# A recorded order of an attention and MLP kernel: three loads for half of a q, and other places for loads, RELUs and copies

## The chip, the cores and the metric

The kernel runs on one core of a Trainium2 chip. The metric is the device time of one execution in microseconds (us), the median of three runs. All products are in bf16 on TensorE with sums in f32; inputs and output are f32 in the chip's main memory.

## What is computed

Two parts, one behind the other. The first is attention without a softmax, for 8 batches of 12 heads, 448 positions and 64 features. The second is an MLP with exact GELU on the 3584 rows that come out.

```python
scores = scale * np.matmul(q, k.transpose(0, 1, 3, 2))       # 448 x 448 for each head
attn = np.maximum(scores, 0.0) ** 2 / S
x = matmul(attn, v)                                          # heads side by side: 3584 x 768
h = x @ w_in                                                 # 768 -> 2048
out = (0.5 * h * (1 + erf(h / sqrt(2)))) @ w_out             # 2048 -> 768
```

## The kernel before

**Engines.** Five engines have instruction streams of their own: TensorE (PE), ScalarE (ACT), VectorE (DVE), GpSimd (POOL) and SyncE (SP). Here POOL issues all loads, with a conversion from f32 to bf16 on the way, in one queue (q0 of the profile). It rotates over eight semaphores, so that each of its DMAs waits for the landing of the eighth before it. SP issues the transposes of batches 2 and later, the stores, and a few copies (q1). Each engine takes its instructions strictly in order, and waits at an instruction whose input or buffer isn't ready.

**Attention.** A batch is cut into three groups of four heads, and a group into seven blocks of 128 keys. I write QK(b.g.i) for the scores of one block: four matmuls (L744, in `add_steps`, L727) into a PSUM buffer "w", of which there are three. A RELU empties that buffer into an SBUF tile a_sq, on ACT (L756) or on DVE (L758); a multiplication on DVE squares it in place (MUL, L765). When a group's seven blocks are squared, an AV (`add_av`, L790) multiplies them with v in 28 matmuls (L805), in seven steps, into another "w" buffer, and two copies bring it to xT on ACT or DVE. Batch 0 does all this in halves of the 448 queries, a and b, two half blocks to an instruction.

**Transposes.** TensorE needs q and k with the features on the partitions. For batches 0 and 1 it transposes them itself (`add_tk` L604, `add_tq` L631) and ACT or DVE copies them out of PSUM. For batches 2 to 7 the DMA engines do it (`add_T_dma`, L659, instructions at L667), and a second arrangement of q is made by two half-swap copies on DVE, or by two DMAs of SP ("qT<-qT").

**MLP.** F1 (`add_f1`, L846, matmuls L857) multiplies one column block m of w_in with xT, six matmuls each, and ACT's GELU empties it. F1 of batches 0 to 3 is done while the attention of later batches runs. The second MLP half goes in seven-product groups (`add_group`, L1148) with sums on DVE (L1170), differences of w_out (`add_tsums`, L1115, at L1120), products (L1191) and results passed on (L1225). F1 of the last four batches is done in blocks of the same kind (`add_blocks`, L1009).

**The order.** Nothing is scheduled when the kernel is built: the string `ORDER` (L86) holds every operation in turn, 1471 words. A word is an engine's letter (P, A, D, G for POOL, S) and the operation's number, counted as the operations are added; Z is a filling operation. `Scheduler.place` (L356) reads it word by word. The word thus sets the order on each engine and also, for RELUs and copies that may go to either, the engine. Whether a wait results, only the chip decides.

The loads of batch 0's q: group 0's first half is loaded ahead of everything by SP, those of groups 1 and 2 by one load each, and the second halves of all three groups by one load `add_q(0, 0, G, HC, NC)` (L1378; G is 3, HC to NC the second half).

The order of the loads in POOL's queue before (q, k, v with batch and group; a and b the halves of batch 0's q; "ident" a small instruction):

```
k0g1 q0g1a k0g2 q0g2a ident q0b(all groups) k1g1 v0g0 k1g0 v0g2 q1g0 q1g1 v0g1 win0 win1 k1g2 q1g2
win2 k2g0 win3 v1g0 win4 q2g0 k2g1 q2g2 q2g1 k2g2 v1g1 v1g2 q3g0 wout0 v2g0 wout1 v2g1 q3g1 k3g0 ...
```

win0 and win1 hold two column blocks of w_in each, win2 to win4 four each; wout0 is one half of w_out, wout1 and wout2 a quarter each. SP issues batch 2's transposes in the order q0 k0 q1 k1 q2 k2.

Of the kernel before, what the change touches and what calls it, by code (L numbers as in the profile page):

```python
# [14 lines left out]
NC = S // KC  # L15
HC = NC // 2
# [70 lines left out]
G0 G1 G3 G4 G1470 G7 A10 D13 A16 G121 P11 G2 P17 D12 D18 G117 P14 P42 D15 P39 G6 A43 P21 A40 P33  # L87
D22 P36 D44 P19 A37 P23 D20 G118 A34 D24 P25 G122 P54 D41 A26 G5 A55 P66 P57 Z1056 D67 A58 P63
P27 P29 A64 P69 D30 P48 D59 P31 A70 D28 D38 P78 A49 P51 D35 P133 G8 A52 D50 P45 D68 A79 P81 D53
A134 D46 P75 D47 G9 D65 A32 P131 A82 D56 P111 D132 A76 P108 D112 P129 G125 A109 D71 P102 P84 D103  # L90
G126 A85 P72 D80 P60 A73 D130 G120 A74 P93 D77 A61 P135 D104 A62 P96 D110 P105 A97 P141 D106 G147
A94 G124 D98 P165 A142 P90 P168 D107 A166 P143 D113 D86 A91 D83 P114 G119 A169 D92 P87 D115 A144
D95 A116 P171 D88 P137 A172 D89 P99 D138 A136 P159 P156 G128 D100 P145 D160 A157 D101 P162 A146
D173 P174 P186 G148 D175 P251 A187 D167 P243 A252 D170 A163 D158 P183 D188 A244 P189 P195 G150
P259 D184 A196 G154 A190 D176 P253 G151 D164 A260 G153 D161 P139 D191 P180 A140 P198 P177 D181
A199 D185 A254 P219 P216 G123 A178 P245 A220 G127 D179 S229 D182 P247 A246 A217 S228 P210 A248
P204 D218 P207 P263 A208 D205 P261 D211 A264 D197 S232 P192 A262 P213 D200 P222 A214 P255 D209
S231 A223 D193 P257 A256 D215 S235 P267 D206 A258 D194 S234 D221 P249 A268 D224 D212 P201 A250
P225 D230 G270 A202 A203 G238 P276 P279 A226 G149 D277 P265 A227 G239 A280 D233 P294 A266 P288
P291 A295 G152 P356 A289 P348 G272 G269 G271 P303 P285 A357 A292 A349 P350 A304 A286 P354 A351  # L100
D287 P312 P300 A355 P318 S399 P362 D281 D313 D296 P364 A363 D319 P370 D278 A301 A365 P358 A371
P315 P306 A359 P282 P352 D307 P360 A353 G241 P376 A361 P368 A377 A283 P366 A369 D284 D302 D236
D293 P372 A367 D290 P374 A373 P378 D390 D316 G274 P327 A379 P297 D391 A328 G273 G155 P333 P339
D314 A334 G240 P382 D298 D305 D317 A340 A375 S398 D308 A299 D320 D329 P330 P324 D417 P309 A325
P380 A383 A331 D310 D311 D392 P342 P321 P336 A381 A337 D332 D418 D341 D419 D326 S402 P384 A322
S401 D393 P387 D396 A385 S405 D394 D400 G407 G242 G237 A323 A343 G409 S386 G275 S404 P443 P446
D335 D420 G408 A444 P421 D395 D344 A447 D338 P449 D388 A450 D397 S389 A422 G412 P452 P345 D445
D346 P437 G411 P423 A453 A438 P440 A347 D424 D403 P455 S542 A441 P425 A456 D439 D442 P473 A426
P470 P461 P427 D454 A471 A474 D462 P429 D428 D457 P464 P479 P476 D430 A480 P431 D448 A465 D451
G414 G415 P433 D472 A477 D432 D562 D406 P467 P458 A468 S435 D469 P485 P491 S545 A486 D434 P509  # L110
D459 A492 S541 P513 A510 D560 A460 D478 D561 P503 S544 A514 P494 P500 D563 P519 A501 D481 D463
P515 A520 D475 A504 A495 D493 P517 D466 D543 S547 D496 D487 P488 A518 P482 A516 D502 S548 G552
P497 P511 D498 S436 G555 D499 P523 G551 A512 D489 A483 G550 A484 G416 P525 A524 D490 D546 G554
P600 G413 P609 P606 G410 D610 P521 D505 A601 A607 P603 P506 D604 A526 A522 P612 P639 D507 P531
A640 P527 G558 D613 D605 A532 D508 G557 P618 A528 P624 P615 D619 P529 S705 S704 A616 P537 S708
# [12 lines left out]
P832 D890 A878 P886 P904 D833 A887 S947 P690 D834 G848 G853 D905 P892 A691 P883 P692 A893 D884
D888 P901 A693 P898 P910 A911 P698 S950 D906 D882 D899 D885 D894 D876 P696 A699 S946 P694 D725
A697 S599 A902 D879 D912 P702 A695 P700 A703 D903 D726 P727 A701 D900 D891 P916 S949 P907 P895  # L130
D917 A908 A728 S948 P928 P913 D929 D909 P731 A914 S953 A896 D915 D918 P729 A897 S951 D930 P925
P922 S952 P919 D926 A923 D730 S579 P931 D927 D732 P934 A920 P733 A921 A932 D924 D935 P735 D734
D736 D933 P940 P937 P955 P737 A956 D936 D743 A941 P739 D738 A938 D744 S741 D942 P747 D939 D740
P958 A748 P970 S742 P943 D959 A971 S954 D746 P961 P964 A944 D1035 P749 A962 D965 A945 D966 P973
P982 D750 P967 P751 A974 A968 D745 D957 D969 D963 D972 P753 A752 P755 A983 D960 D754 D975 P994
P985 P976 A995 D986 P979 P997 D756 D984 P757 A980 A998 D854 D1037 P759 D987 A977 D758 A978 S761
P1015 D981 D855 P988 P1003 A1016 P858 D760 D856 D1027 A989 P860 A1004 A859 P991 P1018 P1012 D861
D999 D1036 A1019 P862 D990 D996 A992 P864 D1038 A1013 D993 D1017 P1021 P1000 D865 D1028 D1020
A1022 D857 A863 P1006 P1009 A1001 P866 A1002 A1007 D1030 D1127 D1005 P1039 P1056 P1041 A1057
# [1420 lines left out]
```

## Time and profile before

| | us |
|---|---|
| median of three runs (lowest, highest) | 366.22 (366.13, 366.34) |
| span of the profiled execution, first to last instruction | 365.2 |
| TensorE busy | 356.2 |
| VectorE busy | 297.5 |
| ScalarE busy | 208.2 |
| GpSimd busy | 64.2 |

The span leaves out what lies around the first and the last instruction, about 1.0 us against the median. In the views below, a line of groups gives the code line, the engine, the operation, output and input, a count, the busy time and the mean of one in ns, and then the idle time ahead of it with what ended it. A line of waits reads: who, waiting for whom, us in total, times, the longest. A line of a timeline or of the chain begins with its start and its length in us; xN is the number of instructions, and [0.23 <-DVE ...] an idle time ahead of it and what ended it. A row of windows gives, for a stretch of the span, the busy us of each engine with the number of its instructions in brackets, the granted clock, the DMA engines' share, and GB/s. A line of DMA issues ends with the median us from issue to landing.

### The profile page before, as it was taken

To read this page: it belongs to the slowest core of one execution; us is meant where nothing else is said; L and a number is where in the kernel's file an instruction comes from. 1 tells how busy PE (TensorE), PEld (TensorE's weight loads), DVE (VectorE), ACT (ScalarE), POOL (GpSimd) and SP (SyncE) were. 2 spreads that over 40 slices of the span, in tenths; PEclk is the share of its full clock that TensorE was granted. 3 is DMA by queue.
4 is the path that set the end of the run, shared out by engine and by line. 5 is a ranking of instruction groups with operands and counts; after the bars stand their busy time and mean duration, and the time that the engine had idled before them with its cause. 6 is when DMAs were issued, how large, how long until landed. Compare 5 with 4: busy or idle time off the path is not lost.

```text
span 365.2 us, 8578 instructions
## 1 busy us (share of the span) xinstructions
PE 356.2 (98%) x3598; PEld 225.4 (62%) x3598; DVE 297.5 (81%) x510; ACT 208.2 (57%) x337; POOL 64.2 (18%) x101
## 2 busy tenths in 40 slices
PE   8799999999999999999999999999999999999996
PEld 4575644455454445555445555799787689788664
DVE  3899784399999988999899999999867847665764
ACT  5998868555767686766766677437027024425310
POOL 8575224160124125014000000000000000000000
PEclk9999999999999999999999999999999999999999
DMA  9999999999999999999792301002021200140223
GB/s 168 199 200 207 198 154 138 191 203 181 186 221 198 197 172 209 219 157 154 132 168 70 95 20 43 3 2 86 3 85 46 88 0 2 45 129 2 85 70 106
DMA packets 73126, 44.12 MB, mean 121 GB/s; under 512 B 38144, under 2 KB 69760, under 8 KB 73088
## 3 DMA queue, kind: packets, MB, share of 16 engines
q0 software_dynamic: 32912, 22.47, 42.7%
q1 hardware_dynamic: 39280, 20.26, 29.0%
q10 hardware_dynamic: 896, 0.85, 0.7%
q8 instruction: 28, 0.46, 0.5%
q14 instruction: 10, 0.08, 0.1%
HBM read 45.61 MB, written 11.01 MB: 155 GB/s over the span
## 4 chain that ended last, share of the span: by engine, by line
PE 78%; DVE 10%; DMA 7%; POOL 2%; issue 2%; ACT 1%; POOLq 0%; DVEq 0%
PE pso L1191 33%; PE pb L1009 18%; PE psh L857 14%; PE ps L744 7%; PE pav L805 6%; DMA win_sb<-in_moe_w_in_dram 5%; DVE a_sq L765 4%; DMA nq<-in_q_dram 2%; DVE t_sb L1120 1%; DVE a_sq L758 1%; DVE s_sb L1170 1%; DVE qT L518 1%; POOL nk L553 1%; ACT a_sq L756 0%; POOL win_sb L481 0%
## 5 line engine op out<-in xcount | busy, mean ns | idle before, releaser
L756 ACT ACTIVATE a_sq<-ps 128x896 bf16<-128x896 f32 (+1 forms) x125 | 110.3, 927 | 33.5 <-PE ps L744 33.4
L765 DVE TENSOR_TENSOR a_sq<-a_sq 128x896 bf16<-128x896 bf16 (+1 forms) x169 | 96.9, 614 | 11.8 <-ACT a_sq L756 11.3
L857 PE MATMUL psh<-xT,win_sb 128*128 128x448 bf16 (+1 forms) x420 | 77.6, 337 | 0.9 <-DMA win_sb<-in_moe_w_in_dram 0.9
L857 PEld LDWEIGHTS <-win_sb 128*128 128x128 bf16 x420 | 38.9, 98 | 37.3 <-issue 9.4
L1046 DVE TENSOR_TENSOR part<-pb,part 128x448 f32<-128x448 f32 x80 | 47.3, 619 | 15.9 <-PE pb L1009 14.2
L1191 PEld LDWEIGHTS <-s_sb 128*128 128x128 bf16 x424 | 40.5, 98 | 26.8 <-issue 2.4
L758 DVE TENSOR_SCALAR a_sq<-ps 128x896 bf16<-128x896 f32 (+1 forms) x44 | 47.1, 1074 | 9.2 <-PE ps L744 9.1
L744 PE MATMUL ps<-qT,kT 64*64 64x448 bf16 (+1 forms) x756 | 47.7, 336 | 1.6 <-ACT qT L520 0.5
L867 ACT ACTIVATE h_sb<-psh 128x448 bf16<-128x448 f32 x64 | 35.0, 552 | 20.8 <-PE psh L857 20.4
L1191 PEld LDWEIGHTS <-h_sb 128*128 128x128 bf16 x312 | 29.4, 98 | 21.6 <-issue 4.6
L1009 PEld LDWEIGHTS <-win_sb 128*128 128x128 bf16 x384 | 36.8, 98 | 2.7 <-issue 0.4
L1191 PE MATMUL pso<-wout_sb,h_sb 128*128 128x384 bf16 x208 | 38.1, 326 | 0.0
L1191 PE MATMUL pso<-t_sb,s_sb 128*128 128x384 bf16 x208 | 38.1, 326 | 0.0
L1191 PE MATMUL pso<-wout_sb,s_sb 128*128 128x384 bf16 (+1 forms) x208 | 37.6, 324 | 0.0
L805 PE MATMUL pav<-a_sq,v_sb 64*64 64x448 bf16 (+1 forms) x756 | 36.7, 329 | 0.6 <-DVE a_sq L765 0.2
L1055 ACT ACTIVATE h_sb<-part 128x448 bf16<-128x448 f32 x48 | 25.4, 575 | 14.6 <-DVE part L1046 14.6
L1225 DVE TENSOR_TENSOR osb<-pso,p_sb 128x384 f32<-128x384 f32 x39 | 21.5, 552 | 14.7 <-PE pso L1191 11.0
L744 PEld LDWEIGHTS <-kT 64*64 64x64 bf16 x756 | 18.8, 105 | 22.3 <-issue 16.3
L805 PEld LDWEIGHTS <-v_sb 64*64 64x64 bf16 x756 | 21.4, 107 | 11.9 <-issue 2.5
L464 POOL DMA_DIRECT2D nq<-in_q_dram x24 | 17.8, 744 | 59.9 <-DMA qT<-nq 55.2
L1009 PEld LDWEIGHTS <-ws 128*128 128x128 bf16 x288 | 27.6, 98 | 1.0
L1055 ACT ACTIVATE h_sb<-pb 128x448 bf16<-128x448 f32 x16 | 8.2, 541 | 29.3 <-PE pb L1009 29.2
(62 smaller groups left out, 327.1 us busy)
## 6 DMA issues: line engine op xcount, KB each, us to landing
nk<-in_k_dram POOLq DMA_DIRECT2D x23, 224.0 KB, 8.1
nq<-in_q_dram POOLq DMA_DIRECT2D x21, 224.0 KB, 7.0
v_sb<-in_v_dram POOLq DMA_DIRECT2D x5, 672.0 KB, 11.6
out_dram<-osb SPq DMA_DIRECT2D x7, 336.0 KB, 2.9
v_sb<-in_v_dram POOLq DMA_DIRECT2D x9, 224.0 KB, 9.9
out_dram<-osb SPq DMA_DIRECT2D x7, 288.0 KB, 3.3
out_dram<-osb SPq DMA_DIRECT2D x8, 240.0 KB, 3.0
win_sb<-in_moe_w_in_dram POOLq DMA_DIRECT2D x8, 192.0 KB, 9.6
```

The costliest lines, as they stand in the source:

```text
L744: nc.tensor.matmul(ps[64 * j : 64 * j + 64, e, x * w : x * w + w], kT[r, g, i * 128 + 64 * j : i * 128 + 64 * j + 64], moving, start=True, ...
L756: A.activation(ar, ps, AF.Relu, scale=c_att)
L758: V.tensor_scalar(ar, ps, c_att, 0.0, op0=mybir.AluOpType.mult, op1=mybir.AluOpType.max,)
L765: V.tensor_mul(box["a2"][:, :, :used], ar, ar)
L805: nc.tensor.matmul(pav[0][o2 : o2 + 64, e, :w], vt[b][r, 2 * g + e, bass.ts(i, D)], box["a2"][r, y, o : o + w], start=(i == 0), stop=(i == ...
L857: nc.tensor.matmul(ph[:, x * n : x * n + n], win_sb[:, kd, bass.ts(m + x, 128)], xT[b][:, kd, c], start=(kd == 0), stop=(kd == KD - 1),)
L867: A.activation(h_ring()[:, m : m + nm, o + c.start : o + c.stop], box[0][:, :S].rearrange("p (x n) -> p x n", x=nm), AF.Gelu,)
L1009: nc.tensor.matmul(bank[name][:, y, z * HS : z * HS + HS], w[:, k, bass.ts(mm, 128)], right()[:, k], start=first and k == 0 and z == 0, st ...
L1046: V.tensor_add(get(to), ps(name), get(other))
L1055: A.activation(h_ring()[:, m : m + 2, o + half[c].start : o + half[c].stop], src().rearrange("p (x n) -> p x n", x=2), AF.Gelu,)
L1191: nc.tensor.matmul(box[bank][:, n0:n1], left()[:, kf], right()[:, kf, n0:n1], start=bool(need) and kf == 0, stop=kf == K2 - 1, skip_group_ ...
L1225: V.tensor_add(out()[:, n0:n1], box[bank][:, n0:n1], other()[:, n0:n1])
```

## The change

The one load of the second halves becomes one for each group:

```diff
     add_v(0, 2, 3)
-    add_q(0, 0, G, HC, NC)
+    for g in range(G):
+        add_q(0, g, g + 1, HC, NC)
     add_win(0)
     add_win(1)
```

Two operations more shift the numbers of those behind them by two. The rest of the diff is a new `ORDER` of 1473 words:

```diff
 ORDER = """
-G0 G1 G3 G4 G1470 G7 A10 D13 A16 G121 P11 G2 P17 D12 D18 G117 P14 P42 D15 P39 G6 A43 P21 A40 P33
-D22 P36 D44 P19 A37 P23 D20 G118 A34 D24 P25 G122 P54 D41 A26 G5 A55 P66 P57 Z1056 D67 A58 P63
...
+G1 A12 D15 G1472 P13 D14 G0 A18 P16 P19 G3 D17 P23 P38 G4 D20 P35 P44 P21 G8 A36 A39 D24 D45 P41
+P25 D22 P27 G7 D46 G9 A42 P56 D26 A57 D28 P31 P68 A69 D37 G2 D40 G120 G123 P71 G119 P65 D32 D43 D66
...
```

It has the same operations. POOL's queue becomes

```
q0g1a ident k0g1 k0g2 q0g2a q0g1b q0g0b q0g2b v0g0 q1g0 k1g1 k1g0 v0g2 v0g1 win0 win1 q1g1 k1g2
win2 win3 q1g2 v1g0 win4 q2g0 k2g1 k2g0 v1g1 q2g1 v1g2 q2g2 v2g0 k2g2 wout1 wout0 v2g1 k3g2 wout2 q3g0 ...
```

and SP's transposes of batch 2 come as q0 k0 k1 q1 q2 k2. DVE has 508 operations where it had 494, ACT 319 where it had 335, SP 74 where it had 72. Around the last AVs of batch 1 (words P203 and P227) the new order reads

```
P194 P212 A266 P209 P259 D195 P269 A260 P251 A270 D210 D187 D199 P267 D211 D190 A213 D232 D208 D193
D214 D196 P203 D223 A204 A268 A252 D226 D217 D220 D205 P227
```

where P194, P212, P209 are QK(1.1.4), QK(1.2.2), QK(1.2.1), P259 to P267 four F1s, D195 and D210 the RELUs of 1.1.4 and 1.2.1, D232 the half-swap of batch 2's q, group 0, D196 the square of 1.1.4 and D220 that of 1.2.4. The two orders are the same, number shift aside, from F1 of batch 3, m=4 on TensorE (240 of its 485 operations), in the last 143 of ACT, 256 of DVE, 35 of SP and 2 of POOL.

More of the change, by code (lines that the diff above doesn't have):

```diff
@@ L92 @@
[L92 to L103, printed above, removed]
@@ new lines @@
+D67 P29 Z1056 A72 G6 G5 P59 G10 D30 P53 P50 G11 P33 A60 A54 G124 G127 P83 P133 D51 P80 G122 G126
+A84 D61 D58 P47 D34 A81 D48 P86 G128 D52 P135 D49 P110 P113 D70 A87 G121 D73 D114 D115 D55 P104
+A111 D136 A105 P77 P74 A78 A75 P62 A63 D134 D79 P95 P131 A76 A64 D106 A96 P107 P98 D132 G130 D108
+P143 P170 P92 D82 A99 P167 D109 D112 G150 A144 A93 D171 D88 D94 A168 P145 G152 G149 S231 P158 D85
+A159 P116 A117 D100 D97 G125 P89 P173 A118 G153 A146 A90 P139 A91 D174 A140 D160 P101 P164 G129
+P161 A102 P137 D138 A103 P245 A165 A246 P253 P188 D175 D166 D172 D162 P176 P185 A189 D169 D177 A186
@@ new lines @@
+P147 G156 A254 P182 P197 P191 A148 P261 D178 P255 A198 A262 A256 D183 P141 D192 D163 P200 P179 G151
+D201 D184 A142 P224 P218 P247 G155 G241 D202 D219 P249 A248 P257 S230 D225 A180 P221 P206 A250 A181
+P215 P263 A258 A207 A222 D216 P265 A264 P194 P212 A266 P209 P259 D195 P269 A260 P251 A270 D210 D187
+D199 P267 D211 D190 A213 D232 D208 D193 D214 D196 P203 D223 A204 A268 A252 D226 D217 D220 D205 P227
+P293 P287 A228 A229 P356 A357 P358 A294 S233 A288 A359 P350 S234 P290 P296 P284 A351 D289 D235 A297
@@ new lines @@
+A291 D298 P364 D285 A365 S237 P352 P372 D238 P278 P281 P317 A353 A373 D282 P366 S236 D318 G240 A367
+P354 D279 P360 A355 D283 A361 P305 P302 P308 P378 D295 A306 A379 D303 P362 P370 D309 P314 D286 A363
+G154 D280 G275 A315 G243 P341 D292 D342 A371 P299 D310 G272 S401 D392 P329 P320 G271 P368 A369 P380
+A381 A321 D330 D300 P382 D301 A383 P335 P326 D319 D393 G274 P311 D304 D327 D322 D316 S400 S404 D331
+D395 P374 G273 S403 A312 G276 A336 P384 A375 D385 D307 P376 P344 P332 A333 A377 D313 D337 P323 P338
@@ new lines @@
+D396 A339 S407 G157 P389 D394 D419 D397 D420 D324 D340 A345 A325 D343 D402 D398 A390 P386 D399 P448
+P439 P457 D387 D422 G409 D346 G414 G244 D334 P425 A458 G277 P423 P454 A449 D328 D405 D421 P347 A440
+A455 A424 P445 D456 P481 A348 A349 P427 A482 D446 G239 S388 G411 D426 A428 D450 P451 P463 D459 A452
+A464 P475 A476 S406 P429 P431 P472 D441 P442 P466 D453 D430 A473 P433 D483 D408 D432 D443 P435 G412
+G242 P487 D447 A467 P469 A470 D444 P460 S544 D488 D436 P478 D434 D477 P493 G415 G410 P515 A479 D480
@@ new lines @@
+D471 D489 A494 A461 S547 A516 P511 D462 G417 P505 D562 D468 D465 P502 P496 A512 A503 A497 P521 G413
+G416 S550 S543 A522 P517 D545 A518 D506 D474 P513 D507 P519 P499 P490 P484 A514 D500 A520 A491 P608
+P602 D504 D485 D498 A609 A486 S546 D495 G554 D492 D548 P525 G557 A526 P523 D501 P527 A603 G553 P611
+P605 A524 A606 D612 A528 P508 P641 P614 A615 P533 D563 D604 S437 S549 A534 P529 P531 D509 A642 D510
+S551 P620 P626 P617 S710 A530 D621 A532 A618 P539 D622 D627 P535 D616 P659 P629 A540 A536 P638 P537
@@ new lines @@
+G560 G418 G556 D643 D610 D639 A660 D619 D613 D564 P566 A630 A538 G559 P541 S438 D607 G555 D628 P632
+P635 A567 A636 D631 A542 P623 S707 P653 D633 P644 D640 S709 P568 D637 D645 A654 A624 A625 D646 D708
+D634 D569 P650 P668 P665 S706 P570 D651 D565 D661 D652 A669 A571 P572 A666 P574 P656 A657 D573 D670
+D584 P662 D663 D655 D582 D575 P647 P771 P765 D583 A766 A648 A772 D664 G716 G717 P576 D577 G552 A649
+P578 S712 S713 D773 D711 D579 D714 G558 P774 P777 P780 P586 P588 A781 A778 D585 D667 D658 S391 A775
@@ new lines @@
+S953 D932 P927 P924 S954 P921 D928 A925 D732 S581 P933 D929 D734 P936 A922 P735 A923 A934 D926 D937
+P737 D736 D738 D935 P942 P939 P957 P739 A958 D938 D745 A943 P741 D740 A940 D746 S743 D944 P749 D941
+D742 P960 A750 P972 S744 P945 D961 A973 S956 D748 P963 P966 A946 D1037 P751 A964 D967 A947 D968
+P975 P984 D752 P969 P753 A976 A970 D747 D959 D971 D965 D974 P755 A754 P757 A985 D962 D756 D977 P996
+P987 P978 A997 D988 P981 P999 D758 D986 P759 A982 A1000 D856 D1039 P761 D989 A979 D760 A980 S763
+P1017 D983 D857 P990 P1005 A1018 P860 D762 D858 D1029 A991 P862 A1006 A861 P993 P1020 P1014 D863
@@ new lines @@
+D1001 D1038 A1021 P864 D992 D998 A994 P866 D1040 A1015 D995 D1019 P1023 P1002 D867 D1030 D1022
+A1024 D859 A865 P1008 P1011 A1003 P868 A1004 A1009 D1032 D1129 D1007 P1041 P1058 P1043 A1059 P1060
+D1010 D1025 D1016 A1012 P870 A1042 D1013 D1061 P1062 P1026 D1044 D1131 D1033 D869 A1027 A1028 P1064
+P1047 D1034 P1045 D1065 P1049 P872 A1063 A1046 D1031 D1048 D1036 P1066 P1052 D1050 D1067 P1069
+P1075 D1053 P1092 D1070 P1055 A1076 P1077 A1093 D1056 D1035 P1094 P1096 D1095 P1079 D1078 P1072
+D873 P1098 A1068 D1073 A1097 A1080 A1074 P1081 D871 P1083 D1082 D1099 S874 S764 A1051 A1054 P1100
@@ new lines @@
+P1133 D1101 D1130 A1057 D1084 P1103 P1086 A1071 D1333 P1150 A1085 D1104 P1106 A1151 D1087 P1089
+A1134 A1105 A1102 P1135 D1090 A1088 P1152 D1107 P1137 D1136 A1108 P1154 D1334 A1091 P1141 A1138
+D1109 P1113 P1139 D1132 D1110 D1111 P1115 D1153 A1114 A1155 D1112 D1140 D1116 D1142 P1117 P1156
+D1243 D1241 P1144 P1119 D1157 D1118 P1169 P1147 P1161 D1120 D1148 D1162 D1145 P1121 D1122 D1242
+P1186 P1158 P1167 P1123 A1168 D1170 P1184 D1159 P1173 A1185 P1164 D1174 P1171 D1187 P1125 D1165
+D1124 P1190 S1127 P1175 D1126 D1191 P1192 P1188 S1128 S875 P1195 D1193 D1176 P1178 A1172 A1189
@@ new lines @@
+A1146 P1181 D1179 A1163 P1198 D1196 A1180 A1166 P1247 D1199 D1335 P1264 A1197 P1245 P1205 D1201
+D1202 D1203 P1262 A1160 A1206 A1143 P1207 A1263 A1194 P1209 D1182 D1208 A1183 A1200 A1149 A1246
+P1211 D1210 A1177 D1204 P1213 D1212 D1214 P1215 D1221 P1217 P1253 P1249 D1222 D1216 D1248 D1218
+P1225 D1223 D1265 S1220 P1227 D1224 D1226 S1219 P1251 P1229 P1266 D1244 D1252 D1336 D1228 P1268
+P1231 A1250 A1267 P1256 D1232 P1270 D1269 D1230 D1254 D1257 P1235 P1233 P1273 P1279 D1236 D1274
+P1296 D1271 P1281 P1298 A1280 A1297 P1259 D1282 P1300 D1234 P1283 P1237 D1260 D1299 A1255 A1301
@@ new lines @@
+A1261 A1284 P1285 P1302 A1258 A1275 P1287 P1304 D1286 D1303 P1276 D1288 P1290 D1277 P1307 D1305
+P1337 D1291 D1308 A1292 P1293 P1310 D1238 A1309 P1339 D1294 S1240 A1338 P1356 A1278 D1340 D1313
+A1295 P1317 D1314 A1318 A1289 P1341 D1315 P1354 P1319 A1355 A1306 D1311 A1272 D1357 D1316 A1312
+P1321 D1320 P1360 A1322 P1323 P1343 P1325 D1324 D1344 D1361 D1407 D1326 P1345 P1362 P1327 P1329
+D1346 D1328 D1363 D1330 P1365 P1348 S1331 S1332 P1351 D1366 P1368 P1358 D1349 A1359 S1239 P1371
+A1367 D1369 P1388 D1405 A1342 A1350 P1409 D1352 P1373 A1410 A1389 A1372 A1347 P1390 P1379 P1392
@@ new lines @@
+D1391 D1374 P1375 P1396 D1406 P1394 P1377 A1353 A1376 P1411 D1395 D1397 P1399 A1398 D1412 P1413
+D1378 D1400 P1415 A1414 A1401 A1393 P1382 D1416 P1417 D1383 D1408 A1384 P1419 D1418 D1380 D1425
+D1420 P1421 P1385 D1422 P1402 D1426 S1424 P1429 D1386 S1423 D1427 A1381 A1370 P1431 A1387 A1430
+A1364 P1433 D1432 P1435 D1434 D1403 D1436 D1428 P1437 A1404 P1439 D1447 D1438 D1445 P1441 D1440
+D1446 S1443 P1449 D1442 S1444 P1451 A1450 P1453 D1452 P1455 D1454 S1466 P1457 D1456 D1448 P1459
+D1458 D1461 S1467 D1460 P1462 P1463 D1464 S1468 S1469 D1465 S1470
```

77 lines of the change are left out of this document (10 added, 67 removed).

## The prediction

> **What bounds the kernel now.** I read the page's head first, then the waits of TensorE, because only time that TensorE gains or loses moves the end.
>
> ```profile
> span 365.2 us, 8578 instructions
> PE 356.2 (98%) x3598; PEld 225.4 (62%) x3598; DVE 297.5 (81%) x510; ACT 208.2 (57%) x337; POOL 64.2 (18%) x101
> ```
> ```profile
> PE psh L857 <- DMA win_sb<-in_moe_w_in_dram: 0.9, 2, 0.5
> PE tp L640 <- DMA nq<-in_q_dram: 0.8, 1, 0.8
> ...
> PE pav L805 <- DVE a_sq L765: 0.2, 1, 0.2
> ```
>
> TensorE is idle for 365.2 − 356.2 = 9.0 us in all, and its waits for loads, the only thing that a better order of loads can remove, are 0.9 + 0.8 us. The table of windows shows the second thing. I cut it where the second-half AV of batch 0's group 1 begins (28.4), near the last AV of batch 1 (53.0), at the first and last AV of batch 2, and at the last ones of batches 3 and 4; the last row but one ends where F1 (the first MLP product) of batch 3, m=7, begins.
>
> ```profile
> core 0: us, PE busy (x) PEld busy (x) DVE busy (x) ACT busy (x) POOL busy (x), PEclk, DMA share, GB/s
> 6.00:28.40 22.40, 19.49 (x507) 14.46 (x511) 20.54 (x41) 20.42 (x31) 15.47 (x23) 1.00 1.39 197
> 28.40:53.00 24.60, 23.73 (x276) 14.02 (x278) 21.59 (x36) 18.66 (x28) 7.89 (x12) 1.00 1.31 186
> 53.00:77.40 24.40, 24.40 (x190) 11.67 (x186) 11.96 (x19) 15.98 (x28) 9.00 (x13) 1.00 1.28 172
> 77.40:94.80 17.40, 17.40 (x180) 9.37 (x174) 17.27 (x27) 11.25 (x17) 4.72 (x8) 1.00 1.33 183
> 94.80:123.50 28.70, 28.34 (x278) 13.73 (x271) 26.93 (x48) 21.77 (x32) 8.83 (x14) 1.00 1.28 207
> 123.50:153.40 29.90, 29.90 (x298) 15.57 (x301) 27.32 (x45) 20.95 (x32) 6.96 (x12) 1.00 1.30 197
> 153.40:177.20 23.80, 23.80 (x240) 12.13 (x233) 21.85 (x38) 15.96 (x25) 5.59 (x10) 1.00 0.90 145
> ```
>
> TensorE is dense in every window after 28.4 (short of 0.87 and 0.36 us in two rows), at full clock. But VectorE (the third busy figure) is nearly as dense: idle 1.86, 3.01, 12.44, 0.13, 1.77, 2.58 and 1.95 us. Only 53 to 77 has room. ScalarE has 2 to 8 us in every row. So VectorE is the engine that can hold TensorE up. The chain of waits says it too: between 80 and 84.5 us it runs through VectorE alone.
>
> ```profile
> 80.25 2.67 DVE a_sq L765 x5
> 82.92 0.60 DVE s_sb L1170
> 83.52 1.01 DVE a_sq L758
> ```
>
> From these rows: a square (L765) is 2.67/5 = 0.534 us of VectorE and a RELU there (L758) 1.01.
>
> **The change, part by part.** *Work that changes its engine.* I counted the operations of both orders by engine. 14 full RELUs and one half RELU go from ScalarE to VectorE.
>
> ```profile
> L756 ACT ACTIVATE a_sq<-ps 128x896 bf16<-128x896 f32 (+1 forms) x125 | 110.3, 927 | 33.5 <-PE ps L744 33.4
> L765 DVE TENSOR_TENSOR a_sq<-a_sq 128x896 bf16<-128x896 bf16 (+1 forms) x169 | 96.9, 614 | 11.8 <-ACT a_sq L756 11.3
> ...
> L758 DVE TENSOR_SCALAR a_sq<-ps 128x896 bf16<-128x896 f32 (+1 forms) x44 | 47.1, 1074 | 9.2 <-PE ps L744 9.1
> ```
>
> So L758 will read x59 and L756 x110. ScalarE loses some 13 us, which buys nothing: TensorE hardly waits for it. VectorE gains 14 × 1.01 + 0.6 = 14.7, and with copies that go both ways (five half xT copies and two half-swaps leave it, q and k copies and two full xT copies come) about 14.1 us net before F1 b3 m7. By my windows: +3.3 up to 28.4 (three RELUs, one of them half, a square, three q or k copies, less three xT halves), +2.7 up to 53.0 (three RELUs), +4.6 up to 94.8 (three RELUs, two xT copies), −0.6, +2.7 and +1.5 (two, none and four RELUs, with sums and swaps shifted between the rows). From F1 b3 m7 on, all five engines issue the same operations in the same order, and TensorE is dense there, so what is late at 177 is late at the end.
>
> *Loads.* The second halves of batch 0's q come in three thirds (g1, g0, g2) instead of one, v and the first two win loads pass q1 g1, the next two pass q1 g2. Two more issues of POOL lie in an engine at 18%. The gains: the 0.75 and the two win waits, 1.7 us at most; I take 0.9, the win waits, since each win load that was waited for moves up by one or two loads, while the nq wait only changes its place. Both ends for this part: −1.7 and 0. Later, wout1 and wout0 are issued before the SP queue has finished batch 2's transposes; see the rivals. I take it as 0 for the forecast, between 0 and +8.
>
> *A, 6 to 36 us.* VectorE gets 3.3 us more, and part of its idle time there is of no use to it, because it is at the very start, behind the first transposes and QK:
>
> ```profile
> 8.63 1.16 DVE L518 COPY kT<-tp 128x896 bf16<-128x896 bf16 x2 [0.35 <-PE tp L612]
> ...
> 10.98 1.09 DVE L758 TENSOR_SCALAR a_sq<-ps 128x896 bf16<-128x896 f32 x1 [0.66 <-PE ps L744]
> 12.31 0.39 DVE L518 COPY qT<-tp 128x448 bf16<-128x448 bf16 x1 [0.24 <-PE tp L640]
> ```
>
> 1.86 − 0.35 − 0.66 − 0.24 = 0.6 us can take work, so 3.3 − 0.6 = 2.7 us overflow ahead of batch 0's last AVs, less the 0.9 of loads: **+1.8**. Ends: −0.9 (all hidden by squares that no AV needs yet) and +3.3.
>
> *B, batch 1's last AVs.* In before, three QKs (x12), four F1 and both AVs follow one another without a wait:
>
> ```profile
> 46.39 0.69 PE ps L744 x12
> 47.08 4.65 PE psh L857 x24
> 51.73 2.77 PE pav L805 x56
> 54.50 0.38 PE ps L744 x8
> ```
> ```profile
> 48.74 3.29 DVE L765 TENSOR_TENSOR a_sq<-a_sq 128x896 bf16<-128x896 bf16 x6
> 52.06 0.97 DVE L518 COPY qT<-qT 64x896 bf16<-64x896 bf16 x2
> ```
>
> An AV waits for each square as it comes to it, not for the whole set:
>
> ```profile
> 94.78 0.54 PE L805 MATMUL pav<-a_sq,v_sb 64*64 64x448 bf16 x5
> 95.55 1.32 PE L805 MATMUL pav<-a_sq,v_sb 64*64 64x448 bf16 x23 [0.23 <-DVE a_sq L765]
> ```
>
> The new order has the same on TensorE: QK(1.1.4, 1.2.2, 1.2.1), F1 ×4, AV g1, AV g2. On VectorE come behind that first QK: RELU(1.1.4), RELU(1.2.1), four squares, batch 2's first half-swap, then squares 1.2.0, 1.1.3, 1.2.2, **1.1.4**, 1.2.5, 1.2.6, 1.2.3, **1.2.4**. From the start of QK(1.1.4): a product and its flight about 0.43, two RELUs 2.02, four squares 2.14, the swap 0.97, four squares 2.14: square 1.1.4 is there at 7.70. TensorE reaches it (fifth of seven steps) at 0.69 + 4.65 + 4/7 × 1.38 = 6.13: it waits 1.57. AV g2 then starts at 7.70 + 3/7 × 1.38 = 8.29, reaches its fifth step at 9.08 and waits for square 1.2.4 (7.70 + 4 × 0.534 = 9.84) 0.76. Sum **+2.3**. Ends: 0 (VectorE never behind, ScalarE's RELUs early) and +4.1 (the AV held for its whole set). Queued behind the swap are those eight squares; were q b2 g0's transpose late, its swap would hold them all.
>
> *C, 54 to 123.* The three RELUs fit into the 12.4 us of room up to 77. What is left is by place, from the same walk with row durations: the first product of batch 0's second MLP half waits for two weight differences (L1120, 0.9 each) and a swap ahead of them on VectorE, 1.0; QK(3.2.3) for its PSUM buffer 0.4; AV b2 g1 0.3; and the 0.23 of the row above goes: **+1.5**, ends −0.2 and +3.
>
> *D, 123 to 177.* 4.2 us are added where VectorE has 2.58 + 1.95 idle. By balance that would be free. By place it isn't, because QK gets its PSUM buffer (three in all) only when the RELU that empties an older one is done, and VectorE takes that RELU in its turn. Worked for one place: the order has QK(5.0.1), QK(5.1.0), AV b4 g2, QK(5.0.6), QK(5.1.3) on TensorE and, on VectorE, squares 4.2.5, 4.2.2, 5.0.5, 5.0.3, then RELU(5.0.1), whose buffer QK(5.1.3) takes.
>
> TensorE needs three QKs (0.19 each) and an AV (1.39), 1.96 us, from QK(5.0.1) to QK(5.1.3); VectorE, just at 4.2.5, needs 4 × 0.534 + 1.01 and 0.1 = 3.25: it waits 1.3. The same count at the others gives QK(4.1.6) 0.8, QK(4.2.0) 0.5, a product behind its passed sum 0.5, QK(5.0.0) 0.7, a product 0.3, QK(5.2.0) 0.3, AV b5 g1 0.6, QK(6.0.0) 0.5: with the 1.3 **+5.5**. Ends: 0 (balance) and +7.
>
> *Switches.* TensorE changes between attention and MLP shapes 6 times less, at about 0.1 (three QKs after F1 took 0.69, two after an AV 0.38, so 0.69 − 0.57): **−0.6**, ends −1 and 0.
>
> Sum: 1.8 + 2.3 + 1.5 + 5.5 − 0.6 = +10.5. On the profiled execution 365.2 + 10.5 = 375.7; the median 366.22 (366.13 to 366.34) has 1.0 more around the span, so 376.7. A measurement tells about 0.2% (0.7 us) from no change.
>
> **Rivals.** (1) *Later room absorbs D.* If RELUs on VectorE run ahead of their turn in D by the room in C, as the balance says, only A, B and half of C stay: 1.8 + 2.3 + 0.8 − 0.6 = +4.3, with 1 of D about 371.5. For it: 53 to 77 has 12.4 us. Against: in-order queues, and C's room ends at 77.
>
> (2) *wout starves the transposes.* Before, wout0 shared the DMA engines with batch 2's last transposes:
>
> ```profile
> wout_sb<-in_moe_w_out_dram POOLq DMA_DIRECT2D x1, 1536.0 KB, 18.1
> ...
> kT<-nk SPq DMA_TRANSPOSE x3, 8.4
> qT<-nq SPq DMA_TRANSPOSE x3, 6.7
> ```
> ```profile
> DMA to landing us min/median/max: 3.0/6.7/14.9
> ```
>
> From issue to landing a transpose takes up to 14.9 instead of the median 6.7. In the new order wout1 and wout0 lie beside almost all six of batch 2. If TensorE's QKs of its groups 1 and 2 wait for that, the difference is 8.2; part of it lies beside F1 of batch 1, so I take +6 on top: 382.7. The Trainium skill ("DMA: Bandwidth & Descriptors", "Queues, rings and completion order") says that a DMA engine goes round its queues packet by packet. By that rule the transposes, with many small packets, would stretch as in this rival; the rows agree with it as far as they go.
>
> (3) *Not slower.* VectorE's room, 23.7 us in the seven rows, takes all 14.1, since every RELU moved has its square soon behind it anyway, and the loads give 1.7 and the switches 0.6: 363.9 at best, 365 with some stalls left. It decides if less than 2 us of the new work stands ahead of a square or RELU that TensorE is waiting for; my count in B alone is over that. The Trainium skill ("Perfetto Trace Analysis", "Identifying the Most-Contended Engine") would have the engine of highest occupancy set what matters; it adds that matmul busy is no good measure of headroom. By its first part TensorE at 98% hides what VectorE gets, and this rival holds; the chain row of 80 to 84.5 speaks against it.
>
> (4) *It doesn't do what it says.* Of batch 1 only q1 g1 falls behind the first win loads; loads alone are then worth 0 and leave A at +2.7: 377.6, inside the forecast.
>
> **How the numbers follow.** Forecast (373.5 to 380, likeliest 376.7) 0.6; rival 1 (368 to 373.5) 0.2; rival 2 (over 380) 0.12; rival 3 0.08, of which 0.06 faster and 0.02 the same. Slower 0.92. 8 in 10 reach from rival 1's middle into rival 2: 370.5 to 382.7.
>
> **What would show it.** Page: L758 x59, L756 x110, VectorE busy about 312. Waits of TensorE: L805 and L744 for a_sq of VectorE with some 3 and 4 us in place of 0.2 and none, win_sb near 0. Windows: TensorE no longer dense around AV b1 g1 and between F1 b2 and F1 b3 m7; after that a plain shift. A: AVs of batch 0 late by 2 us. Wrong if TensorE waits for qT or kT of DMA (rival 2), if its idle time before 60 us is under 2 us more (A, B), or if F1 b3 m7 begins before 183 (D).

## The result

The changed kernel takes 380.36 us (median of four runs, 379.48 to 381.91) where the kernel before takes 366.27 (366.13 to 366.34): a ratio of 1.0383, 95% interval 1.0355 to 1.041. That is +14.1 us; forecast were +10.5, to 376.7, in a range of 370.5 to 382.7. The time is in the range, but 0.4 us above the band of 373.5 to 380 that had a chance of 0.6, and so in that of rival (2), which had 0.12. The profiled execution is the fastest of the four, with a span of 377.7 us for its 379.48. Wherever a run has both numbers they lie about 1.8 us apart, for the kernel before too (364.5 and 366.29); the profile of before that the prediction used, with its 365.2, was thus some 0.7 us longer than most.

The head of the page after:

```profile
span 377.7 us, 8566 instructions
...
PE 359.6 (95%) x3598; PEld 227.9 (60%) x3598; DVE 309.0 (82%) x522; ACT 196.4 (52%) x321; POOL 65.5 (17%) x103
...
L754 ACT ACTIVATE a_sq<-ps 128x896 bf16<-128x896 f32 x110 | 97.4, 920 | 44.0 <-PE ps L742 43.7
...
L756 DVE TENSOR_SCALAR a_sq<-ps 128x896 bf16<-128x896 f32 (+1 forms) x59 | 62.3, 1067 | 12.4 <-PE ps L742 12.0
```

TensorE's idle time has gone from 9.0 to 18.1 us, with the same 3598 matmuls. Its busy time has grown too, by 3.4 us, of which 2.5 is on QK (47.7 to 50.2) and 1.0 on AV (36.7 to 37.7), though a single matmul of them takes no longer (337 ns after 336, 330 after 329). VectorE has 15 RELUs more (29 went to it and 14 to ScalarE; code lines are smaller by two). What TensorE waits for:

```profile
PE ps L742 <- DVE a_sq L756: 6.8, 10, 1.2
PE pav L803 <- DVE a_sq L763: 2.6, 6, 0.7
PE spin L1367 <- DVE zero L1350: 1.0, 1, 1.0
PE pso L1189 <- DVE osb L1223: 0.7, 1, 0.7
```

The waits for loads of win and nq have gone. In their place are waits of QK for a PSUM buffer that a RELU on VectorE empties (6.8 us in ten pieces), and of AV for squares (2.6). VectorE's own list names what is new there, a transpose:

```profile
DVE qT L516 <- DMA qT<-nq: 4.6, 2, 3.5
```

To see where the time went I gave each operation of TensorE its length in a dense stretch (QK 0.19, F1 1.14, AV 1.33, a group of products 1.4), and summed what lies beyond that up to marks which both orders share. I call this the excess. Changes between attention and MLP shapes are in it. The second and third columns are the starts of the mark in the two profiles; each excess is counted from the mark above.

| up to | before | after | excess, before | excess, after | added | forecast |
|---|---|---|---|---|---|---|
| AV b1 g1 | 51.7 | 53.9 | 10.1 | 10.9 | 1.1 (0.2 at the start) | A 1.8 |
| QK(2.0.5), behind AV b1 g2 | 56.5 | 59.0 | 0.2 | 2.5 | 2.3 | B 2.3 |
| AV b2 g0 | 77.4 | 78.9 | 0.9 | 3.8 | **2.9** | none |
| AV b3 g2 | 123.5 | 130.3 | 2.9 | 3.5 | 0.6 | C 1.5 |
| F1 b3, m=4 | 175.0 | 187.2 | 1.6 | 7.0 | 5.4 | D 5.5 |

The profile of before spends its extra 0.7 us in the rows of A and C. The run below that leaves out squares of batch 4 in the kernel before has the same orders up to AV b3 g2 and a span of 364.4; against its profile A's row adds 1.4 and C's 0.9.

Marks alone would mislead: AV b2 g2 begins 9.0 us later and AV b4 g0 only 5.4, because the orders put other F1s and products between them. From F1 b3, m=4 on every mark is 12.2 us later to the end (AV b7 g2, for one):

```profile
233.58 1.52 PE L805 MATMUL pav<-a_sq,v_sb 64*64 64x448 bf16 x28
```
```profile
245.78 1.52 PE L803 MATMUL pav<-a_sq,v_sb 64*64 64x448 bf16 x28
```

The first line is of before, the second of after.

**B** looks as worked out. In the chain of waits after, from 48.95 us:

```profile
48.95 2.09 DVE a_sq L756 x2
51.04 2.14 DVE a_sq L763 x4
...
53.21 0.39 DVE qT L516
...
53.61 0.39 DVE qT L516
...
54.01 4.38 DVE a_sq L763 x8
...
58.44 0.76 PE pav L803 x12
```

From top to bottom: two RELUs, four squares, a half-swap, eight squares, and only then AV g2's last three steps: the list of the prediction, with 0.8 for the half-swap instead of 0.97. **D's** worked place, QK(5.1.3) behind QK(5.0.6), is in TensorE's timeline:

```profile
163.96 0.39 PE L742 MATMUL ps<-qT,kT 64*64 64x448 bf16 x4
165.47 0.38 PE L742 MATMUL ps<-qT,kT 64*64 64x448 bf16 x4 [1.12 <-DVE a_sq L756]
```

**The term that was missed** is at 70 us. VectorE's timeline, then TensorE's:

```profile
64.73 0.79 DVE L516 COPY qT<-qT 64x896 bf16<-64x896 bf16 x2 [1.06 <-DMA qT<-nq]
...
70.72 0.79 DVE L516 COPY qT<-qT 64x896 bf16<-64x896 bf16 x2 [3.54 <-DMA qT<-nq]
71.54 3.08 DVE L756 TENSOR_SCALAR a_sq<-ps 128x896 bf16<-128x896 f32 x3
```
```profile
72.68 0.38 PE L742 MATMUL ps<-qT,kT 64*64 64x448 bf16 x4 [1.19 <-DVE a_sq L756]
73.68 0.38 PE L742 MATMUL ps<-qT,kT 64*64 64x448 bf16 x4 [0.62 <-DVE a_sq L756]
74.68 0.38 PE L742 MATMUL ps<-qT,kT 64*64 64x448 bf16 x4 [0.61 <-DVE a_sq L756]
```

A half-swap of batch 2's q stands on VectorE waiting 3.54 us for its transpose. Three RELUs stand behind it, each holding one of the three PSUM buffers, so three QKs come one RELU apart. TensorE's waits name the RELU; its cause is one step further back, and in another engine's queue.

### The profile page after: what moved, and what is told of

The parts are those of the page before. It is cut to its first block, busy times and chain, and to the rows that moved or that the text cites. A ratio compares the mean times of both kernels' runs of the same rounds, so it can differ in the third digit from the quotient of the medians.

```text
span 377.7 us, 8566 instructions
## 1 busy us (share of the span) xinstructions
PE 359.6 (95%) x3598; PEld 227.9 (60%) x3598; DVE 309.0 (82%) x522; ACT 196.4 (52%) x321; POOL 65.5 (17%) x103
## 4 chain that ended last, share of the span: by engine, by line
PE 72%; DVE 24%; issue 1%; DMA 1%; ACT 1%; DVEq 0%
PE pso L1189 26%; PE pb L1007 17%; PE psh L855 15%; DVE a_sq L763 11%; PE ps L742 6%; DVE a_sq L756 6%; PE pav L803 5%; DVE qT L516 2%; DVE s_sb L1168 2%; PE pso L1293 1%; DVE osb L1223 1%; DMA q<-in_q_dram 1%; DVE xT L516 1%; ACT a_sq L754 0%; DVE wout_sb L1118 0%
## 5 line engine op out<-in xcount | busy, mean ns | idle before, releaser
L754 ACT ACTIVATE a_sq<-ps 128x896 bf16<-128x896 f32 x110 | 97.4, 920 | 44.0 <-PE ps L742 43.7
L756 DVE TENSOR_SCALAR a_sq<-ps 128x896 bf16<-128x896 f32 (+1 forms) x59 | 62.3, 1067 | 12.4 <-PE ps L742 12.0
L742 PE MATMUL ps<-qT,kT 64*64 64x448 bf16 (+1 forms) x756 | 50.2, 337 | 8.1 <-DVE a_sq L756 6.8
L803 PE MATMUL pav<-a_sq,v_sb 64*64 64x448 bf16 (+1 forms) x756 | 37.7, 330 | 3.5 <-DVE a_sq L763 2.6
L742 PEld LDWEIGHTS <-kT 64*64 64x64 bf16 x756 | 19.8, 105 | 30.6 <-issue 25.1
L551 POOL DMA_DIRECT2D nk<-in_k_dram x23 | 16.4, 717 | 66.4 <-DMA kT<-nk 64.6
L518 ACT CAST xT<-pav 128x448 bf16<-128x448 f32 (+1 forms) x40 | 18.1, 490 | 11.9 <-PE pav L803 10.3
```

The lines of the kernel that those rows point to most:

```text
L742: nc.tensor.matmul(ps[64 * j : 64 * j + 64, e, x * w : x * w + w], kT[r, g, i * 128 + 64 * j : i * 128 + 64 * j + 64], moving, start=True, ...
L754: A.activation(ar, ps, AF.Relu, scale=c_att)
L756: V.tensor_scalar(ar, ps, c_att, 0.0, op0=mybir.AluOpType.mult, op1=mybir.AluOpType.max,)
L803: nc.tensor.matmul(pav[0][o2 : o2 + 64, e, :w], vt[b][r, 2 * g + e, bass.ts(i, D)], box["a2"][r, y, o : o + w], start=(i == 0), stop=(i == ...
```

## The experiments

All are made from the changed kernel unless said otherwise. Theory S: the loss is a sum of separate waits at the places above. Where a change only concerns the order, the diff is of words of `ORDER`, or of POOL's queue in the short names used above; "..." stands for what is left out.

**Squares first (B).** Five squares whose RELUs are done go ahead of the two RELUs that wait for QK (two of them ahead of one RELU more).

```diff
-D216 P265 A264 P194 P212 A266 P209 P259 D195 ... D210 D187 D199 P267 D211 D190 A213 D232 D208 D193
+D187 D199 D216 P265 A264 P194 P212 A266 P209 P259 D190 D193 D208 D195 ... D210 P267 D211 A213 D232
```

> The changed kernel with five squares (1.1.1, 1.1.5, 1.1.2, 1.1.3, 1.2.0) ahead of two RELUs on VectorE instead of behind them, nothing else. Theory S (the loss is a sum of separate stalls, each worth its own size at the end): the two waits of AV b1 g1 and g2, 1.57 and 0.70 us, go, and the kernel takes 378.1 where the changed one took 380.4. Rival T (batch 2's transposes land late and set when its half-swaps, and the RELUs behind them, come): the AV waits go but the wait around 71 us grows by the same amount, so 380 within 0.7.

Measured: 380.39 us (379.99 to 381.19), no gain. Rival T holds. In its profile (of the 381.19) B's excess falls from 2.5 to 0.5 us, as S said. But between QK(2.0.5) and AV b2 g0 it grows from 3.8 to 6.3. Its chain of waits there begins with a transpose under way for 15.73 us:

```profile
55.78 15.73 DMA qT<-nq
...
72.35 3.10 DVE a_sq L756 x3
```

TensorE comes earlier to a wait whose end the DMA sets, and the longest of its waits there is 1.92 us in place of 1.19. About 1.2 us of the growth is something else: the granted clock, the share of full speed that TensorE gets, is 0.5 from 74.6 to 78.0 us in this profile. Two of the other executions, with a mean clock of 0.999, took 379.99 and 380.51 and thus gained nothing either. So B and the missed term aren't independent.

**wout behind.** wout1 and wout0 go behind v2 g1 and k3 g2 in POOL's queue, wout0 now first.

```diff
-... v2g0 k2g2 wout1 wout0 v2g1 k3g2 wout2 q3g0 ...
+... v2g0 k2g2 v2g1 k3g2 wout0 wout1 wout2 q3g0 ...
```

> The changed kernel with the loads of wout1 and wout0 moved behind k3 g2 in GpSimd's queue, nothing else. Both theories: if wout beside batch 2's transposes makes them late, the half-swaps wait less than 4.6 us for the DMA and the 2.4 us of TensorE behind the RELUs there shrink to under 1: 377.5 to 378.5. Rival D (the transposes are late because of the other loads, or because they are issued late): no change, 380 within 0.8.

Measured: 376.30 us (376.23 to 376.48), 4.1 less than the changed kernel's median, 3.3 less between the two profiled runs (spans 377.7 and 374.4), and steadier. The excess before AV b2 g0 falls from 3.8 to 0.9, that of before; the other stages stay within 0.3. The DMA issues between 40 and 62 us, of after and then of this kernel (the last number is the median us to landing):

```profile
wout_sb<-in_moe_w_out_dram POOLq DMA_DIRECT2D x1, 1536.0 KB, 24.3
...
qT<-nq SPq DMA_TRANSPOSE x3, 14.3
kT<-nk SPq DMA_TRANSPOSE x3, 12.7
```
```profile
wout_sb<-in_moe_w_out_dram POOLq DMA_DIRECT2D x1, 1536.0 KB, 12.7
...
qT<-nq SPq DMA_TRANSPOSE x3, 6.6
kT<-nk SPq DMA_TRANSPOSE x3, 10.4
```

Beside wout, q's transposes take more than twice as long and k's a fifth longer (medians of three each), and the one big load of wout twice as long. Taking it away gives the missed term back: it is rival (2), in small.

**Both.**

> Both edits of the two runs before together. Theory S: their gains add, 2.3 + 2.5, so 375.6. Theory T: the order of squares alone gives nothing but with early transposes it gives its 2.3 too, so also 375.6, where the sum of the two single gains would be only 2.5. Rival D: 378 or more.

The edit is the two diffs above together. Measured: 375.86, 375.87, 375.64 and 380.43 us (median 375.86). The number is near the expected 375.6, but not for its reasons: moving wout alone had given 4.1 already, and the squares add 0.4 of their 2.3, so even with wout out of the way they aren't worth their size. The profile is of the 380.43. There the first half-swap waits 1.67 us for its transpose with six squares behind it, which leaves B an excess of 1.6; and TensorE waits 2.63 us for a transpose of batch 3's k, behind which the granted clock is 0.5 from 112.9 to 116.3 us (the last run below has the same).

**The split alone**, in the kernel before: the one load of q as three, all else as it was.

```diff
-    add_q(0, 0, G, HC, NC)
+    for g in range(G):
+        add_q(0, g, g + 1, HC, NC)
```

> The kernel before with nothing but the three-way split of the load of q's second halves, all other loads and all orders as before. All theories: the loads of q come 1 to 2 us earlier for the first third and at the same time for the last; the wait of 0.75 us for nq goes or halves, two more DMAs push the later ones by a semaphore: 366 within 0.7.

Measured: 366.16 us, ratio 1.0001 (0.999 to 1.0012). The three loads by themselves are worth nothing; TensorE's wait for nq is 1.0 instead of 0.8.

**Less work for VectorE in D**, on top of wout behind: eight squares of batch 4 are left out (their attention isn't squared).

```diff
+                if blocks[0][:3] in ((4, 1, 1), (4, 1, 2), (4, 1, 3), (4, 1, 4), (4, 1, 5),
+                                     (4, 2, 0), (4, 2, 1), (4, 2, 3)):
+                    return
                 ar = box["a2"][:, :, :used]
```

> The kernel of the run with wout1 and wout0 moved behind (376.3 us), with eight squares of batch 4 left out of VectorE's work (4.1.1 to 4.1.5, 4.2.0, 4.2.1, 4.2.3: the attention of these blocks is then not squared); 8 x 0.534 = 4.3 us less for VectorE between 130 and 155 us, everything else as it was. Theory V (the waits of TensorE for PSUM buffers between 140 and 180 us, 5.1 us in all, come from VectorE being behind with its queue): those up to QK(5.1.3), 0.8 + 0.7 + 0.7 + 1.3 us, go, and most of the later ones shrink: 372 to 373.2. Rival P (three PSUM buffers are too few whoever empties them, or the waits belong to ScalarE): within 0.5 of 376.3.

Measured: 374.03 us, 2.3 less (373.41, 373.95, 374.10 and 377.78; why one is long is open). In the profile (span 371.6 against 374.4) the excess between AV b3 g2 and AV b4 g2 falls from 3.2 to 0.7, so those waits were VectorE's, not too few PSUM buffers as such. The rest of D barely changes, 3.8 to 3.5; QK(5.1.3) still waits 0.87 us, since the squares ahead of RELU(5.0.1) are other ones. Theory V is right for the first half of D, and its gain was put 1 to 2 us too high.

> The kernel before with the same eight squares left out. Theory V: TensorE waits for nothing there, so nothing is gained: 366.3 within 0.5. Rival P expects the same; if the kernel before also gained 2 us or more, VectorE would bound it as a whole, and the loss of the changed kernel would follow from its 14 us of added work, whatever its place.

Measured: the kernel before with the same squares left out takes 366.38 us, ratio 1.0006 (0.9995 to 1.0017). There VectorE's 4.3 us cost nothing.

**Computing and loads crossed.** First the new orders of TensorE, ScalarE and VectorE with the loads and batch 2's transposes in the order before, then the reverse.

```diff
-q0g1a ident k0g1 k0g2 q0g2a q0g1b q0g0b q0g2b v0g0 q1g0 k1g1 k1g0 v0g2 v0g1 win0 win1 q1g1 k1g2 ...
+k0g1 ident q0g1a k0g2 q0g2a q0g1b q0g0b q0g2b k1g1 v0g0 k1g0 v0g2 q1g0 q1g1 v0g1 win0 win1 k1g2 ...
```

> The changed kernel's orders on TensorE, ScalarE and VectorE with the order of loads and of batch 2's transposes as before (only the small ident instruction stays at its new place, and the load of q stays in three). Theory S2 (loads cost 3 to 4 us through late transposes, compute the other 10): 376.5 to 377.5, by early transposes, with up to 0.9 us of win waits back. Rival L (the new computing order needs its new order of loads): waits of TensorE for nq, nk or win of 2 us and more, and 379 or more.

Measured: 379.99 us (379.57 to 380.98): rival L. The excess before AV b2 g0 is 0.9, so transposes are in time, but up to AV b1 g1 it is 3.1 us higher than in the changed kernel. TensorE waits for the load of batch 1's q, group 0:

```profile
17.09 0.96 PE L638 MATMUL tp<-ident,nq 112*64 112x112 bf16 x16 [2.08 <-DMA nq<-in_q_dram]
```

The other 1.0 us comes behind it: the granted clock is 0.5 from 15.8 to 22.7 us, and these 16 transposes take 0.96 us where they take 0.58 in the changed kernel.

The reverse, in the kernel before:

```diff
-k0g1 q0g1a k0g2 q0g2a ident q0b(all groups) k1g1 v0g0 ... k2g2 v1g1 v1g2 q3g0 wout0 v2g0 wout1 ...
+q0g1a ident k0g1 k0g2 q0g2a q0g1b q0g0b q0g2b v0g0 ... v2g0 k2g2 wout1 wout0 v2g1 k3g2 wout2 q3g0 ...
```

> The kernel before's orders on TensorE, ScalarE and VectorE with the changed order of loads and of batch 2's transposes. Theory S2: the transposes are late here too; the old order has 4.6 us idle on VectorE behind its second half-swap, but its squares of batch 2 stand behind it, so 368 to 374, with waits of TensorE for qT, kT or a_sq between 55 and 75 us. Rival L: waits in batch 0 and 1 for nq and nk before 36 us, which the old order asks for earlier, of 2 us or more. A rival that gives the loads no part in the loss: 365.4 to 366.5.

Measured: 376.80 us (376.06 to 378.30), more than S2 allowed: the new loads alone cost the old order 10.6 us. VectorE's timeline, and TensorE's (whose first line, ahead of the wait, is for comparison):

```profile
66.43 0.81 DVE L516 COPY qT<-qT 64x896 bf16<-64x896 bf16 x2 [8.96 <-DMA qT<-nq]
```
```profile
58.38 2.44 PE L855 MATMUL psh<-xT,win_sb 128*128 128x448 bf16 x12
66.92 1.32 PE L742 MATMUL ps<-qT,kT 64*64 64x448 bf16 x8 [6.09 <-DVE qT L516]
68.17 4.50 PE L855 MATMUL psh<-xT,win_sb 128*128 128x448 bf16 x12
```

The excess before AV b2 g0 is 9.0 us higher than in the kernel before: 6.1 is the wait, and 2.9 the slow stretch behind it. The granted clock is 0.5 from 65.5 to 72.4 us, and two F1s there take 4.50 us instead of 2.44.

So neither part's loss is its own. The new computing order uses batch 2's q later (its first QK of group 1 starts at 67.62 us, that of the kernel before at 59.12) and hides most of what the new loads delay; and it needs batch 1's first q as early as the new loads bring it.

**Eight RELUs back to ScalarE**, on top of wout behind: 1.0.1, 1.0.4, 1.1.4, 1.2.1, 4.1.0, 4.1.4, 4.2.0, 5.0.1, for instance

```diff
-P768 P789 A790 P671 G561 P783 D782 D776 D769
+P768 A769 P789 A790 P671 G561 P783 D782 D776
```

> The kernel with wout1 and wout0 moved behind (376.3 us), with eight RELUs given back to ScalarE, each shortly behind its QK in ScalarE's queue: 1.0.1, 1.0.4, 1.1.4, 1.2.1, 4.1.0, 4.1.4, 4.2.0, 5.0.1, chosen because they stand on VectorE ahead of a square or a PSUM buffer that TensorE waits for. Theory S (place decides): the waits of AV b1 g1 and g2 (2.3 us), of batch 1's QKs (0.6 to 1) and most of those at QK(4.1.6), QK(5.0.0) and QK(5.1.3) (2.8) go, 370.0 to 371.5. Rival W (work decides: TensorE is late by VectorE's total, of which this takes 8.1 of 14 us): nearly all of it comes back, 368.5 or less, and it would not matter which RELUs are taken.

Measured: 372.32 us (371.85 to 373.82), 4.0 less; S had 5 to 6. The profile is of the 373.82. D's excess falls from 7.0 to 4.0. B's rises from 2.5 to 3.7, for a reason that VectorE's timeline shows:

```profile
53.66 0.79 DVE L516 COPY qT<-qT 64x896 bf16<-64x896 bf16 x2 [3.03 <-DMA qT<-nq]
54.46 4.38 DVE L763 TENSOR_TENSOR a_sq<-a_sq 128x896 bf16<-128x896 bf16 x8
```

VectorE is early now, and stands at the half-swap with eight squares behind it.

**26 RELUs back**, straight behind their QKs, on the same base, each in the manner of

```diff
-P795 ... D796
+P795 A796 ...
```

> The same base (376.3 us), but with all 26 full RELUs of batches 1 to 6 given to ScalarE that the kernel before had there and the changed kernel had on VectorE, each straight behind its QK in the order; 26 us less on VectorE, 21 more on ScalarE, which is then busy some 58%. Rival W: VectorE no longer bounds anything, 366 to 370. Theory S: in-order ScalarE then has RELUs ahead of GELUs and xT copies for which F1 and AV wait, so stalls come back in other places; no gain over the run with eight, and by following the order 380 to 387.

Measured: 385.62 us (384.60 to 386.57), 9.3 **more** than the base, as S said. VectorE is busy 284.7 us and ScalarE 216.1 of 382.9; neither looks loaded on the page, yet TensorE waits 4.9 us for F1's buffers alone:

```profile
PE psh L855 <- ACT h_sb L865: 4.9, 8, 1.3
PE ps L742 <- ACT a_sq L754: 3.0, 5, 0.9
PE pav L803 <- ACT a_sq L754: 2.2, 3, 0.8
PE ps L742 <- DVE a_sq L756: 2.1, 4, 1.1
```

By the order, GELUs stand behind RELUs in ScalarE's queue. Rival W, the total of VectorE, is refuted: with 25 us less of it the kernel is slower.

**The kernel before, mended** by seven small moves (four RELUs to the other engine, three exchanges) besides the split.

```diff
-D105 ... A285 ... A45 ... A219 ...
+A105 ... D285 ... D45 ... D219 ...
```

> The kernel before with the load of q in three, RELUs 0.2.0b/0.2.1b on ScalarE and 0.0.6a, 1.2.4, 2.0.2 on VectorE, and three pairs of neighbours exchanged (an xT copy of batch 0, the RELU of 2.0.1, a half-swap of batch 4). What is left to win there is TensorE's 4 us or so of early waits. If the early waits for ps and pav can be had by such small moves: 365.2 to 365.8; if they only change place, as at the AVs of batch 1: 366.2 within 0.4.

Measured: 366.10 us, ratio 0.9985 (0.9964 to 1.0006). Not told from no change; no version here beats the kernel before beyond doubt.

**The half-swap last**, on top of the eight RELUs:

```diff
-A213 D232 D208 D193 D214 D196 P203 D223 A204 A268 A252 D226 D217 D220 D205 P227
+A213 D208 D193 D214 D196 P203 D223 A204 A268 A252 D226 D217 D220 D232 D205 P227
```

> The kernel with eight RELUs given back to ScalarE (372.3 us), with the half-swap of batch 2's q, group 0, moved on VectorE from ahead of the eight last squares of batch 1 to behind them. Theory H (that half-swap, waiting 3.0 us for its transpose in the profile of that run, holds the squares for which AV b1 g1 and g2 wait): TensorE's waits there, 3.7 us in that profile, shrink to 0.5 to 1; QK(2.0.5), which needs the half-swap, waits 0.5 instead: 370.0 to 371.0. Rival Q (QK(2.0.5) follows AV b1 g2 at once and needs the half-swap as early as before): the wait only moves to QK(2.0.5), 372.3 within 0.7.

Measured: 370.42, 371.74, 374.03 and 375.15 us (median 372.88): inconclusive as a time. The profile, of the 374.03, shows H at its place, B's excess 3.7 to 0.4. But now TensorE is 3 us earlier at batch 3, and the wait comes there (second line: AV b3 g0 behind it):

```profile
109.86 0.57 PE L742 MATMUL ps<-qT,kT 64*64 64x448 bf16 x8 [2.06 <-DMA kT<-nk]
110.26 2.58 PE L803 MATMUL pav<-a_sq,v_sb 64*64 64x448 bf16 x28
```

A transpose of batch 3's k isn't there. TensorE wants it at 107.8 us, where the run with wout behind came to it at 110.67; and it was under way for 12.73 us to 109.81, where it had taken 8.64 to 107.87. What made it slower isn't shown. Behind the wait the granted clock is 0.5 from 110.5 to 113.9 us, and the AV takes 2.58 us instead of 1.33. The two shorter executions, 370.42 and 371.74, have a mean clock of 1.000, the two longer ones 0.995; so they probably escaped this stretch, and perhaps the wait, but only one execution of a kernel has a profile.

## Why the prediction was right, point by point

- **The sign and the engine** were right: TensorE's new idle time is nearly all behind VectorE, and the load waits of 0.9 went as forecast. Its waits for a_sq of VectorE are 2.6 us at AV and 6.8 at QK, where I had some 3 and 4. L758 x59 and L756 x110 came out to the piece; VectorE's busy time is 309.0 and not 312: the RELUs grew by 15.2 (47.1 to 62.3), so the rest fell by 3.7, where I had 0.6.
- **A** was 1.8 and measured 1.1, or 1.4 against the shorter profile of the same orders; the last AVs of batch 0 begin 0.6 to 1.2 us later, where I had 2. That more of the new work hides behind VectorE's early idle time is a guess; no run here tests A alone.
- **B** was right in size and place, 2.3 for 2.3. But it wasn't worth 2.3 at the end: the run with squares first gained nothing, and with wout out of the way the squares gave 0.4.
- **C** was 1.5 and measured 0.6 (0.9 against the shorter profile): the wait of a product for the weight differences, put at 1.0, doesn't appear.
- **D** was right, 5.4 for 5.5. The list of places holds nearly one by one (QK(4.1.6) 0.8, a product 0.7, QK(5.0.0) 0.7, QK(5.1.3) 1.3 over dense, AV b5 g1 0.6, QK(6.0.0) 0.6; QK(4.2.0) had none); that the places' errors cancel to 0.1 is luck. Leaving out squares takes 2.5 us of it away. Rival (1), balance, failed: VectorE had the room on average.
- **The switches**, −0.6, can't be seen by themselves; they are inside the measured sums.
- **The step that failed** is the term of wout beside batch 2's transposes, "I take it as 0 for the forecast". It costs 2.9 us in the profiled run and 3.3 to 4.1 when measured by moving wout behind. I had it as rival (2), through TensorE's waits for qT or kT; it came through VectorE's queue, and half as large.
- **The total.** The median lies 3.6 us over the forecast. Of these, 2.0 are in the two profiles, which differ by 12.5: the missed 2.9 and what A and C lack partly cancel, so that the total is nearer than its terms. The other 1.6 is that the profile of before was 0.7 us longer than its median and that of after 0.9 shorter.
- **Rival (4)**, that the loads alone do nothing, is only true of the split. The other loads cost the old computing order 10.6 us.

## What to carry to other kernels

In a kernel of in-order engines, count not how much work an engine gets but what stands behind each piece: eight chosen RELUs given back won 4.0 us, 26 lost 9.3. A wait saved ahead of a late transfer is given back there, so a change of order has to be tested together with the loads that it was made for. When a profile names the engine that holds a PSUM buffer, look one step further back for what that engine was standing at. And read the granted clock behind a long wait: in both crossed runs a clock of 0.5 made up about a third of what TensorE lost there.

## What the runs showed of the hardware

- Transposes on SP's queue took a median of 14.3 and 12.7 us to landing beside 1536 KB of wout, and 6.6 and 10.4 without it. The Trainium skill ("DMA: Bandwidth & Descriptors", "Queues, rings and completion order") has DMA engines go round their queues packet by packet; wout's own landing, 24.3 us beside them and 12.7 later, agrees with it, though no run here tells this from another way of sharing.
- From 7 us on to 2 us before the end the granted clock is 1.0 in nine of the fourteen profiles; in the other five it falls to 0.5 for 3.4 or 6.8 us at a time. For all five waits of TensorE of 1.92 us and more (1.92, 2.06, 2.08, 2.63 and 6.09 us) such a stretch begins in the wait or at most 1.1 us behind its end; of the 18 waits between 1.1 and 1.9 us one has it. With the stretch the wait costs more than its own length: 2.06 us became 3.4 (half-swap last), and 6.09 became 9.0 (old computing order, new loads).
- A kernel can scatter by several us from one execution to the next where a transpose sets a wait: 370.42 to 375.15 in the last run, while the one with wout behind kept within 0.25.
